# A lightning-attention and expert-mixture kernel: two more chunks laid out in DRAM, weight blocks read from the input, a block of sums turned on VectorE, PSUM pairs alternating

## The chip, the cores and the metric

The kernel runs on one core of one Trainium2 chip. The metric is device microseconds (us) of one execution. The kernel before took a median of 1186.92 us over 4 runs (1186.15 to 1188.08). Engines are named TensorE (PE; its weight loads are PEld), VectorE (DVE), ScalarE (ACT), POOL (GpSimd) and SyncE (SP, which issues nearly all DMAs). A line number L843 is a line of the kernel before.

## The reference

Two stages in float32. The first is attention with a decaying state, for 4 batches, 8 heads, 768 positions and head width 64; the second sends the 3072 resulting rows of 512 through 4 experts and adds them up with gates:

```python
# attention, per block of positions, state kv of 64x64 a head
intra = ((qb @ kb.T) * Dmask) @ vb
inter = (qb * lam_pow) @ kv_state
out   = intra + inter
kv_state = lam_block * kv_state + (kb * rev_pow).T @ vb

# experts: x is 3072x512, w1[e] 512x1024, w2[e] 1024x512
p = domain_probs / (domain_probs.sum(-1, keepdims=True) + 1e-09)
for e in range(4):
    h = np.maximum(x @ w1[e], 0.0)
    out += p[:, e:e + 1] * (h @ w2[e])
```

## The kernel before

**Chunks and groups.** The attention works in chunks of 128 positions, 6 a batch, 24 in all (n = 0 to 23, batch b = n // 6, chunk c = n % 6). Eight chunks make a group of 1024 rows, x transposed in `xT`; there are three groups g. The 12 units (g, e) of the expert stage follow one another. While TensorE does the second product (h @ w2) of one unit, it does the first product (x @ w1) of the next between, and steps of the next group's attention go in among them.

**Fast products.** Products are cut into 2x2 blocks and done with 7 products of blocks instead of 8 (M1 to M7, a Winograd scheme): some factors are plain blocks of a matrix, the others sums of blocks. `A_OF` names the factor of each product: A11, A12 and A22, for M1, M2 and M4, are plain blocks of w1; S1 to S4 are sums. Each block product is again cut into 7 inner ones (`INNER`), so that each outer factor has four inner blocks and four inner sums. In the first product (`first_product`, L821) two PSUM banks, g1 and g3, take the inner products by turns and VectorE or ScalarE adds them into blocks `m`. The second product of groups 0 and 1 is cut once (`second_product`, L882, banks q01, q02, q11, q12); in the last group it is nested twice (`nested_product`, L1084) with results `sums`, held transposed: features in partitions, rows in the free dimension.

**Prepared operands.** POOL makes the sums ahead of time, as chores from a list (`pump`) with an estimate of its own busy time, and SP stores what it made. For w1, `inner_w1` writes to `w1_ops[e, m]` seven blocks of 128x256, in the order M1, M7, M6, M5, M3, M2, M4: block 0 and blocks 5 and 6 are copies of the outer factor, blocks 1 to 4 are inner sums. `inner` (L167) stores them with three DMAs; `own_w1` (L1189) does it for expert 1, whose first use is straight from SBUF. `feed` (L748) loads them again: one DMA for x (`xs_in`, L756) and one for w1 (`ws_in`, L758), 896 KB each, one product ahead, into two buffers each. There are 70 such products, from 189 us on.

**Chunks by DRAM.** To make scores, q and k of a chunk are needed with the head dimension in partitions. `turn` (L519) does it for most chunks on TensorE: 4 transposes for q and 4 for k into PSUM (L529), copied to SBUF by ScalarE (L534, L535). For the chunks that `ACROSS` names, chunks 2 to 5 of batches 2 and 3, `bring_across` rearranges q and k within DRAM beforehand (32 DMAs a batch, DRAM to DRAM, in runs of 128 bytes, L367), one at a time between other DMAs (`trickle`); `load_across` (L384) then loads tiles that VectorE turns in blocks of 32x32, in place (L516). k is loaded in its natural layout too, for the state update; in the other path the same tile of k serves both.

**The end.** In the last unit (expert 3 of the last group) products are in the order `SEQ3` = M1, M3, M5, M7, M6, M2, M4. M2 is taken plain (`plain_product`, L1032, bank pM). After M6 the outer blocks are joined: `to_join` (L987) queues copies of sums to PSUM on ScalarE (`bring`) and additions on VectorE (`add`), done one step at a time. The results of blocks M3, M5, M2 and M4 are turned back to rows in partitions by `give` (L1010): TensorE transposes (L1018, 4 for each half of the rows), a copy by ScalarE (L1022), a store by SP (L1024). `after_last` says at which step each is given: M3 during product M2, M5 and M2 during product M4. M4 itself ends the kernel (`turn_end`, `turned_product`).

**PSUM pairs.** A nested product uses a pair of banks. Its pair is chosen by the product's number i in the expert, `i % 2` (three pairs, `i % 3`, in the last expert, which has no first product beside it). There are seven products an expert.

Of the kernel before, what the change touches and what calls it, by code (L numbers as in the profile page):

```python
# [22 lines left out]
def kernel(  # L23
# [30 lines left out]
    nc = tc.nc  # L54
# [4 lines left out]
    P = nc.NUM_PARTITIONS  # L59
# [4 lines left out]
    G = CPG * C  # L64
    NG = NTOK // G
    Q = G // 4
    DH = DOUT // 2
    W = 512
# [15 lines left out]
    MS = ("M1", "M2", "M3", "M4", "M5", "M6", "M7")  # L84
    A_OF = {"M1": "A11", "M2": "A12", "M3": "S4", "M4": "A22", "M5": "S1", "M6": "S2", "M7": "S3"}
# [5 lines left out]
    def small(name):  # L91
        return pool.tile([P, W], FP32, name=name, tag="t")
# [34 lines left out]
    w1_ops = dram.tile([E, 7, P, 7, 256], FP32, name="w1_ops")  # L127
# [9 lines left out]
    chores, queue, late, results, made = [], [], [], [], set()  # L137
    LEFT = 1

    def store(f):  # L140
        queue.append((busy[0] + 2, f))
# [22 lines left out]
        while what not in made:  # L164
            pump(force=True)

    def inner(eng, what, to, blk, ops, at):  # L167

        b = {n: blk[:, i, j * 256:(j + 1) * 256] for n, (i, j) in at.items()}
        s = stage.tile([P, 4, 256], FP32, name="ops", tag="st")  # L170
        for i, (name, x, y, op) in enumerate(ops):
            b[name] = s[:, SLOT[name]]
            tt(eng, b[name], b[x], b[y], op)
        store(lambda: (
            nc.sync.dma_start(out=to[:, 0], in_=blk[:, 0, 0:256]),
            nc.sync.dma_start(out=to[:, 1:5], in_=s[:]),
            nc.sync.dma_start(out=to[:, 5:7], in_=blk[:, 1].rearrange("p (a f) -> p a f", a=2)),
            made.add(what),
        ))

    SLOT = {"S3": 0, "S2": 1, "S1": 2, "S4": 3, "T3": 0, "T2": 1, "T4": 2, "T1": 3}
    S_OPS = (
# [5 lines left out]
        ("T4", "B21", "T2", ALU.subtract),  # L188
    )

    def inner_w1(e, m, blk):
        at = {"A11": (0, 0), "A21": (0, 1), "A12": (1, 0), "A22": (1, 1)}
        inner(nc.gpsimd, ("w1", e, m), w1_ops[e, MS.index(m)], blk, S_OPS, at)

    def inner_x(eng, g, m, blk):
        at = {"B11": (0, 0), "B12": (0, 1), "B21": (1, 0), "B22": (1, 1)}
# [156 lines left out]

    ACROSS = {2: 2, 3: 2}
    across = dram.tile([B, 2, P, NHP, NCH * 4, 32], FP32, name="across")
    pieces = []

# [76 lines left out]
    m = 1  # L436
# [311 lines left out]
    def feed(g, e, m):  # L748
        if (g, e, m) in fed:
            return  # L750
        while ("x", g, m) not in made and background:
            rest(force=True)
        until(("x", g, m))
        until(("w1", e, m))
        xs = stream.tile([P, 7, 256], FP32, name="xs_in", tag="x")
        nc.sync.dma_start(out=xs[:], in_=x_ops[g, MS.index(m)])  # L756
        ws = stream.tile([P, 7, 256], FP32, name="ws_in", tag="w")
        nc.sync.dma_start(out=ws[:], in_=w1_ops[e, MS.index(m)])  # L758
        fed[g, e, m] = {i: xs[:, X_AT[i]] for i in X_AT}, {i: ws[:, W1_AT[i]] for i in W1_AT}


# [213 lines left out]
        x = sums[a][:, 2 * k:2 * k + 2].rearrange("p k t -> p (k t)")  # L975
        tt(nc.vector, x, x, there[b, k][:], ALU.add)

    def joined(m=None):

        while m in apart:  # L980
            take(aside, True)
        while joins and (m is None or any(m in x for x, _ in joins)):
            joins.pop(0)[1]()
            if m is None:
                return

    def to_join(m):  # L987

        def steps(*work):
            for fs in work:  # L990
                joins.append(([x[1] for x in fs if x[0] == add], lambda fs=fs: [x[0](*x[1:]) for x in fs]))

        if m == "M3":
            steps(
                [(bring, "M1", 0, "q01")], [(bring, "M1", 1, "q02"), (add, "M6", "M1", 0)], [(add, "M6", "M1", 1)],
            )
        if m == "M5":
            join("M3", "M5")
            join("M2", "M1")
        if m == "M6":  # L1000
            steps(
                [(bring, "M6", 0, "s0")], [(bring, "M6", 1, "s1"), (add, "M7", "M6", 0)], [(add, "M3", "M6", 0)],
                [(bring, "M7", 0, "q11"), (add, "M7", "M6", 1)], [(bring, "M7", 1, "q12"), (add, "M3", "M6", 1)],
                [(add, "M4", "M7", 0)], [(add, "M4", "M7", 1)], [(add, "M5", "M7", 0)], [(add, "M5", "M7", 1)],
            )
# [4 lines left out]
    def give(m, t, tags, dds=(0, 1)):  # L1010

        joined(m)
        i, j = RESULT[m]
        p, o = bank(tags[t % len(tags)], "yp"), small("y")
        w = len(dds) * P
        for x, dd in enumerate(dds):
            for s in range(2):
                nc.tensor.transpose(  # L1018
                    out=p[:, s * w + x * P:s * w + (x + 1) * P], in_=sums[m][:, 2 * dd + t, s * P:(s + 1) * P],
                    identity=ident[:],  # L1020
                )
        nc.scalar.copy(out=o[:, 0:2 * w], in_=p[:, 0:2 * w])  # L1022
        r, d = LAST * G + j * W + t * 256, i * DH + dds[0] * P
        nc.sync.dma_start(  # L1024
            out=out[r:r + 256, d:d + w].rearrange("(s p) d -> p s d", p=P),
            in_=o[:, 0:2 * w].rearrange("p (s d) -> p s d", s=2),
        )


    PLAIN = E - 1, "M2"  # L1030
# [158 lines left out]
    def own_w1(m):  # L1189

        c = w1_now[1][A_OF[m]]
        b = {f"A{i + 1}{j + 1}": c[j][:, i * 256:(i + 1) * 256] for i in range(2) for j in range(2)}
        s = stage.tile([P, 4, 256], FP32, name="ops", tag="st")
        for n, x, y, op in S_OPS:
            b[n] = s[:, SLOT[n]]
            tt(nc.gpsimd, b[n], b[x], b[y], op)
        store(keep_own(("w1", 1, m), w1_ops[1, MS.index(m)], (
            ((0, 1), c[0][:, 0:256].unsqueeze(1)), ((1, 5), s[:]), ((5, 7), c[1].rearrange("p (a f) -> p a f", a=2)),
        )))
        return {i: b[A_OF[i]] for i in A_OF}  # L1200

    def keep_own(what, to, pieces):
        return lambda: ([nc.sync.dma_start(out=to[:, x:y], in_=of) for (x, y), of in pieces], made.add(what))
# [163 lines left out]
    def pause_till(i, x):  # L1367
# [13 lines left out]

    fill3 = [(e, m, k) for e in range(E) for m in SEQ3 for k in range(4)]
    after_last = {
        "M2": (None,) * 5 + (("M3", 0), ("M3", 1)),
        "M4": (("M5", 0), ("M5", 1), ("M2", 0), ("M2", 1)),
    }
    steps = attention(1)
    PACE = 1.0, 1.4, 1.0
    for at, (g, e) in enumerate(units):
# [14 lines left out]
        for i in range(7):  # L1404
# [8 lines left out]
                    out=gate_bc, in_=gate_rows[:, ahead[1]].partition_broadcast(P),  # L1413
                )
            if nested:
                b = nested_product(e, SEQ3[i], (("q01", "q02"), ("q11", "q12"), ("g1", "g3"))[i % (2 if ahead else 3)])
                if i < 6 and (e, SEQ3[i + 1]) != PLAIN:
                    inner_sums(e, SEQ3[i + 1])
            else:
                b = second_product(g, e, SEQ2[i], banks)  # L1420
# [4 lines left out]
            a = []  # L1425
            if ahead:
                a = first_product(*ahead, SEQ[i], blocks, ("g1", "g3"))
            if (e, SEQ3[i]) == END:
                b[6:6] = [lambda: (give("M4", 1, ("s0", "s1"), (1,)), turn_end(1, "q11"))]
                b[5:5] = [lambda: (give("M4", 0, ("s0", "s1"), (1,)), turn_end(0, "q12"))]  # L1430
            if not ahead:
# [6 lines left out]
            for x, part in enumerate(order):  # L1438
# [12 lines left out]
                if nested and ahead and x in (1, 3) and fill3:  # L1451
                    feed3(*fill3.pop(0))
                if turned_back and x > 0:
                    y = turned_back.pop(0)
                    if y:
                        give(*y[:2], ("s0", "s1"), *y[2:])
                if x == 0 and at * 7 + i >= 6 and fill:
                    feed(*fill.pop(0))
                if at == 0 and x == 0 and i < AHEAD:
# [36 lines left out]
```

## Time and profile before

| what | value |
|---|---|
| median of 4 runs | 1186.92 us (1186.15 to 1188.08) |
| the profiled execution | 1186.15 us |
| its span on the chip | 1184.4 us |
| TensorE busy | 1176.9 us |
| VectorE, POOL, ScalarE busy | 790.4, 630.0, 275.0 us |
| DMA | 324.23 MB, mean 274 GB/s |
| granted TensorE clock | 1.0 |

The span is what the profile sees, from the first to the last instruction; 1.75 us of the profiled execution lie around it. Matmul rows overlap in the profile (each lasts longer than the distance to the next start), so a stretch of them is timed from start to start. A row of a timeline has the start, the time it takes, the engine, the line, the operation, out<-in, shapes and how many instructions were merged, and in brackets the idle time before it and what ended that. A row of waits has the waiting engine and tile, what ended the wait, the total in us, how many there were and the longest. POOL and VectorE work side by side: a VectorE addition of two 128x512 tiles in SBUF lasts 0.68 us in some places and up to 1.36 us in stretches where POOL adds tiles too. The DMA line of the slices is the mean busy share of 16 DMA engines in tenths.

### The profile page before, as it was taken

The page shows a single profiled execution, that of the slowest core. Times are in us where ns is not written, and L with a number is a line of the kernel's source. Part 1 is how long each engine was busy: PE and PEld are TensorE (multiplying, and loading weights), DVE is VectorE, ACT ScalarE, POOL GpSimd, SP SyncE. Part 2 cuts the span into 40 slices and gives each one's busy share as a digit, 9 for nine tenths or more (in the row PEclk, how much of TensorE's full clock was granted, in tenths as well). Part 3 has the DMA queues.
Part 4 walks back from the last instruction along what each step waited for, and adds up shares of the span by engine and source line. Part 5 has one row for each costly group of instructions (what it writes and reads, how often), then busy time and mean ns, then how long its engine had stood idle before and what let it go on. Part 6 is the DMA issues. An engine that isn't in the chain of part 4 may idle for free.

```text
span 1184.4 us, 17886 instructions
## 1 busy us (share of the span) xinstructions
PE 1176.9 (99%) x6567; PEld 1023.5 (86%) x6567; DVE 790.4 (67%) x1329; ACT 275.0 (23%) x502; POOL 630.0 (53%) x600
## 2 busy tenths in 40 slices
PE   9999999999999999999999999999999999999998
PEld 8888888888888888888888888888888888888887
DVE  6785785567478757647856764764665676777784
ACT  3332122112211201211220120121243342341332
POOL 2756258349457800055253655425684683783884
PEclk9999999999999999999999999999999999999999
DMA  9698799999999997899997989898986657566542
GB/s 228 197 286 250 242 304 306 346 334 339 368 358 327 326 305 222 246 303 310 302 310 241 286 294 318 276 329 275 307 296 244 254 189 276 205 240 245 213 160 90
DMA packets 261927, 324.23 MB, mean 274 GB/s; under 512 B 117296, under 2 KB 203216, under 8 KB 261840
## 3 DMA queue, kind: packets, MB, share of 16 engines
q1 hardware_dynamic: 252288, 320.40, 81.5%
q10 hardware_dynamic: 9552, 2.69, 1.1%
q8 instruction: 52, 0.85, 0.3%
q14 instruction: 35, 0.29, 0.1%
HBM read 237.69 MB, written 89.54 MB: 276 GB/s over the span
## 4 chain that ended last, share of the span: by engine, by line
PE 94%; DVE 2%; SPq 2%; DMA 1%; issue 0%; ACT 0%; ACTq 0%; DVEq 0%
PE pg L843 39%; PE q L897 32%; PE pq L1104 13%; PE pc L1234 2%; PE op L579 2%; PE sp L551 1%; SPq L123 1%; PE pM L1234 1%; DVE m L95 1%; PE op L574 1%; PE op L587 1%; PE pM L1039 1%; SPq L341 0%; DMA vn<-in_v_dram 0%; SPq L118 0%
## 5 line engine op out<-in xcount | busy, mean ns | idle before, releaser
L843 PE MATMUL pg<-xs_in,ws_in 128*128 128x256 f32 x1960 | 469.7, 379 | 0.5 <-DVE m L95 0.5
L843 PEld LDWEIGHTS pg<-xs_in,ws_in 128*128 128x128 f32 x1960 | 371.3, 190 | 52.2 <-DVE m L95 1.5
L95 DVE TENSOR_TENSOR m<-pg,m 128x512 f32<-128x512 f32 x451 | 307.9, 687 | 105.9 <-PE pg L843 98.6
L897 PE MATMUL q<-w2t,hS 128*128 128x256 f32 x1024 | 243.4, 380 | 0.0
L897 PEld LDWEIGHTS q<-w2t,hS 128*128 128x128 f32 x1024 | 193.2, 190 | 27.0 <-issue 0.2
L913 DVE SCALAR_TENSOR_TENSOR acc<-q,gate,acc 128x256 f32<-128x256 f32 x192 | 92.5, 482 | 168.9 <-PE q L897 168.8
L897 PE MATMUL q<-w2t,m 128*128 128x256 f32 x768 | 182.7, 381 | 0.0
L897 PEld LDWEIGHTS q<-w2t,m 128*128 128x128 f32 x768 | 144.8, 190 | 20.5 <-issue 0.3
L855 ACT ACTIVATE m<-m 128x512 f32<-128x512 f32 x132 | 82.9, 630 | 281.5 <-DVE m L95 278.0
L95 POOL TENSOR_TENSOR m<-m,xT 128x512 f32<-128x512 f32 x64 | 80.7, 1277 | 71.7 <-ACT m L855 54.0
L95 POOL TENSOR_TENSOR kn<-kn,s_decay 128x512 f32<-128x512 f32 x20 | 23.2, 1158 | 140.1 <-DMA across<-in_k_dram 78.9
L95 DVE TENSOR_TENSOR sums<-pq,sums 128x256 f32<-128x256 f32 x153 | 64.4, 422 | 47.4 <-PE pq L1104 40.1
L851 ACT COPY m<-pg 128x512 f32<-128x512 f32 x88 | 51.6, 586 | 174.9 <-PE pg L843 172.5
L1104 PE MATMUL pq<-acc,w2t 128*128 128x256 f32 x352 | 86.6, 379 | 0.0
L95 POOL TENSOR_TENSOR ops<-w2b 128x256 f32<-128x256 f32 x24 | 18.4, 787 | 115.3 <-DMA w2b<-in_moe_w_dram 107.6
L1104 PEld LDWEIGHTS pq<-acc,w2t 128*128 128x128 f32 x352 | 66.8, 190 | 9.3 <-issue 0.3
L95 POOL TENSOR_TENSOR acc<-hT,hT 128x512 f32<-128x512 f32 x32 | 40.3, 1273 | 30.7 <-PE pq L1104 28.9
L95 POOL TENSOR_TENSOR w2o<-w2b 128x512 f32<-128x512 f32 x32 | 40.6, 1291 | 24.7 <-DMA w_ops<-w1b 14.4
L786 ACT ACTIVATE m<-m 128x512 f32<-128x512 f32 x44 | 27.7, 630 | 103.4 <-DVE m L95 103.3
L95 DVE TENSOR_TENSOR m<-m,m 128x512 f32<-128x512 f32 x56 | 48.8, 872 | 0.0
L95 DVE TENSOR_TENSOR hS<-m,m 128x512 f32<-128x512 f32 x56 | 43.6, 781 | 4.9 <-ACT m L855 4.9
L95 POOL TENSOR_TENSOR acc<-hT,acc 128x512 f32<-128x512 f32 x32 | 40.7, 1273 | 7.4 <-PE pq L1104 5.4
(157 smaller groups left out, 1362.9 us busy)
## 6 DMA issues: line engine op xcount, KB each, us to landing
xs_in<-x_ops SPq DMA_DIRECT2D x70, 896.0 KB, 6.1
ws_in<-w_ops SPq DMA_DIRECT2D x70, 896.0 KB, 8.7
w2t<-w_ops SPq DMA_DIRECT2D x66, 256.0 KB, 6.6
w2t<-w_sums SPq DMA_DIRECT2D x64, 256.0 KB, 3.7
w_ops<-ops SPq DMA_DIRECT2D x28, 512.0 KB, 5.7
w2t<-in_moe_w_dram SPq DMA_DIRECT2D x48, 256.0 KB, 3.4
w2b<-in_moe_w_dram SPq DMA_DIRECT2D x32, 256.0 KB, 6.0
w_sums<-w2o SPq DMA_DIRECT2D x16, 512.0 KB, 4.5
```

The costliest lines, as they stand in the source:

```text
L95: eng.tensor_tensor(out=o, in0=a, in1=b, op=op)
L123: by.dma_start(out=to[:, :, r], in_=of[:, :, r])
L551: nc.tensor.matmul(out=sp[r][:, ac * C:(ac + 1) * C], lhsT=hc(kT)[half[r], ac], rhs=hc(qT)[half[r], ac], start=True, stop=True,)
L579: nc.tensor.matmul(out=op[r][half[x], a * C:(a + 1) * C], lhsT=vn[:, 4 * r + 2 * a + x], rhs=hc(st[r])[:, 2 * a + x], start=(first and a = ...
L786: nc.scalar.activation(out=o[:], in_=o[:], func=AF.Relu)
L843: nc.tensor.matmul(out=p[:, j * 256:(j + 1) * 256], lhsT=ws[i][:, j * P:(j + 1) * P], rhs=xs[i], start=(fresh and j == 0), stop=True, skip ...
L851: nc.scalar.copy(out=new[at][:], in_=p[:])
L855: nc.scalar.activation(out=new[at][:], in_=new[at][:], func=AF.Relu)
L897: nc.tensor.matmul(out=p[:, s * DH:(s + 1) * DH], lhsT=h[A_OF[m]][:, c * 256 + s * P:c * 256 + (s + 1) * P], rhs=fed2[g, e, m][uu][:, c], ...
L913: nc.vector.scalar_tensor_tensor(out=o, in0=x, scalar=w, in1=o, op0=ALU.mult, op1=ALU.add)
L1104: nc.tensor.matmul(out=p[:, 0:256], lhsT=fed3[e, m, x // 2][:, x % 2, c * P:(c + 1) * P], rhs=b[B_OF[i]][:, c * 256:(c + 1) * 256], start= ...
L1234: nc.tensor.matmul(out=p[:, s * 256:(s + 1) * 256], lhsT=a[c][:, f:f + P], rhs=b[:, c, j * 256:(j + 1) * 256], start=(s == 0 and c == 0 an ...
```

## The change

Four things are changed.

1. `ACROSS` has batch 2 from chunk 0 on: chunks 12 and 13 are rearranged in DRAM as well, ten in all. The 32 rearranging DMAs of batch 2 move 6 chunks (96 KB each) where they moved 4 (64 KB).
2. For M1, M2 and M4 (`RAW`), the copies of plain blocks are no longer stored to `w1_ops`: only the four sums are, in one DMA instead of three. `feed` loads such a tile in three DMAs, blocks 0, 5 and 6 from the input w1 itself. Where all three stores remain, the sums go first.
3. `give_across` takes the place of `give` for block M3: VectorE turns 32x32 blocks of `sums` into a tile `y`, and eight DMAs of 64 KB, in runs of 128 bytes, put them at their places in the output (six from SP, two from ScalarE's queue). It is given two steps earlier, a half of the features at a time, and forces the joins up to that half alone.
4. The pair of banks of a nested product goes by the number of the product over all experts, `(at * 7 + i) % 2`, except in the last expert, which keeps `i % 3`.

In the changed order of instructions TensorE has 24 transposes fewer (16 for the two chunks, 8 for M3), ScalarE 6 copies fewer, VectorE 8 transposes more (four of 128x512, four of 128x256) and SP 40 DMAs more.

```diff
@@ -164,19 +164,17 @@
         while what not in made:
             pump(force=True)
 
-    def inner(eng, what, to, blk, ops, at):
+    def inner(eng, what, to, blk, ops, at, whole=True):
 
         b = {n: blk[:, i, j * 256:(j + 1) * 256] for n, (i, j) in at.items()}
         s = stage.tile([P, 4, 256], FP32, name="ops", tag="st")
         for i, (name, x, y, op) in enumerate(ops):
             b[name] = s[:, SLOT[name]]
             tt(eng, b[name], b[x], b[y], op)
-        store(lambda: (
-            nc.sync.dma_start(out=to[:, 0], in_=blk[:, 0, 0:256]),
-            nc.sync.dma_start(out=to[:, 1:5], in_=s[:]),
-            nc.sync.dma_start(out=to[:, 5:7], in_=blk[:, 1].rearrange("p (a f) -> p a f", a=2)),
-            made.add(what),
-        ))
+        pieces = [(to[:, 1:5], s[:])]
+        if whole:
+            pieces += (to[:, 0], blk[:, 0, 0:256]), (to[:, 5:7], blk[:, 1].rearrange("p (a f) -> p a f", a=2))
+        store(lambda: ([nc.sync.dma_start(out=x, in_=y) for x, y in pieces], made.add(what)))
 
     SLOT = {"S3": 0, "S2": 1, "S1": 2, "S4": 3, "T3": 0, "T2": 1, "T4": 2, "T1": 3}
     S_OPS = (
@@ -188,9 +186,11 @@
         ("T4", "B21", "T2", ALU.subtract),
     )
 
+    RAW = ("M1", "M2", "M4")
+
     def inner_w1(e, m, blk):
         at = {"A11": (0, 0), "A21": (0, 1), "A12": (1, 0), "A22": (1, 1)}
-        inner(nc.gpsimd, ("w1", e, m), w1_ops[e, MS.index(m)], blk, S_OPS, at)
+        inner(nc.gpsimd, ("w1", e, m), w1_ops[e, MS.index(m)], blk, S_OPS, at, m not in RAW)
 
     def inner_x(eng, g, m, blk):
         at = {"B11": (0, 0), "B12": (0, 1), "B21": (1, 0), "B22": (1, 1)}
@@ -353,7 +353,7 @@
 
 
 
-    ACROSS = {2: 2, 3: 2}
+    ACROSS = {2: 0, 3: 2}
     across = dram.tile([B, 2, P, NHP, NCH * 4, 32], FP32, name="across")
     pieces = []
 
@@ -755,7 +755,14 @@
         xs = stream.tile([P, 7, 256], FP32, name="xs_in", tag="x")
         nc.sync.dma_start(out=xs[:], in_=x_ops[g, MS.index(m)])
         ws = stream.tile([P, 7, 256], FP32, name="ws_in", tag="w")
-        nc.sync.dma_start(out=ws[:], in_=w1_ops[e, MS.index(m)])
+        if m in RAW:
+            i, j = int(A_OF[m][1]) - 1, int(A_OF[m][2]) - 1
+            src = moe_w1[e, j * 256:(j + 1) * 256, i * W:(i + 1) * W]
+            nc.sync.dma_start(out=ws[:, 0], in_=src[0:P, 0:256])
+            nc.sync.dma_start(out=ws[:, 1:5], in_=w1_ops[e, MS.index(m), :, 1:5])
+            nc.sync.dma_start(out=ws[:, 5:7], in_=src[P:].rearrange("p (a f) -> p a f", a=2))
+        else:
+            nc.sync.dma_start(out=ws[:], in_=w1_ops[e, MS.index(m)])
         fed[g, e, m] = {i: xs[:, X_AT[i]] for i in X_AT}, {i: ws[:, W1_AT[i]] for i in W1_AT}
 
 
@@ -975,11 +982,11 @@
         x = sums[a][:, 2 * k:2 * k + 2].rearrange("p k t -> p (k t)")
         tt(nc.vector, x, x, there[b, k][:], ALU.add)
 
-    def joined(m=None):
+    def joined(m=None, k=None):
 
         while m in apart:
             take(aside, True)
-        while joins and (m is None or any(m in x for x, _ in joins)):
+        while joins and (m is None or any(m == x and k in (None, y) for to, _ in joins for x, y in to)):
             joins.pop(0)[1]()
             if m is None:
                 return
@@ -988,7 +995,7 @@
 
         def steps(*work):
             for fs in work:
-                joins.append(([x[1] for x in fs if x[0] == add], lambda fs=fs: [x[0](*x[1:]) for x in fs]))
+                joins.append(([(x[1], x[3]) for x in fs if x[0] == add], lambda fs=fs: [x[0](*x[1:]) for x in fs]))
 
         if m == "M3":
             steps(
@@ -1025,6 +1032,25 @@
             out=out[r:r + 256, d:d + w].rearrange("(s p) d -> p s d", p=P),
             in_=o[:, 0:2 * w].rearrange("p (s d) -> p s d", s=2),
         )
+
+    halved = {}
+
+    def give_across(m, dd, t):
+
+
+        joined(m, dd)
+        i, j = RESULT[m]
+        if t == 0:
+            halved[m, dd] = small("y")
+        o = halved[m, dd]
+        nc.vector.transpose(out=o[:, t * 256:(t + 1) * 256], in_=sums[m][:, 2 * dd + t])
+        r, d = LAST * G + j * W, i * DH + dd * P
+        for a in range(4 * t):
+            by = nc.scalar if a == 1 else nc.sync
+            by.dma_start(
+                out=out[r:r + W, d + a * 32:d + (a + 1) * 32].rearrange("(b p) d -> p b d", p=32),
+                in_=o[a * 32:(a + 1) * 32].rearrange("p (b d) -> p b d", d=32),
+            )
 
 
     PLAIN = E - 1, "M2"
@@ -1194,9 +1220,10 @@
         for n, x, y, op in S_OPS:
             b[n] = s[:, SLOT[n]]
             tt(nc.gpsimd, b[n], b[x], b[y], op)
-        store(keep_own(("w1", 1, m), w1_ops[1, MS.index(m)], (
-            ((0, 1), c[0][:, 0:256].unsqueeze(1)), ((1, 5), s[:]), ((5, 7), c[1].rearrange("p (a f) -> p a f", a=2)),
-        )))
+        pieces = [((1, 5), s[:])]
+        if m not in RAW:
+            pieces += ((0, 1), c[0][:, 0:256].unsqueeze(1)), ((5, 7), c[1].rearrange("p (a f) -> p a f", a=2))
+        store(keep_own(("w1", 1, m), w1_ops[1, MS.index(m)], pieces))
         return {i: b[A_OF[i]] for i in A_OF}
 
     def keep_own(what, to, pieces):
@@ -1381,8 +1408,8 @@
 
     fill3 = [(e, m, k) for e in range(E) for m in SEQ3 for k in range(4)]
     after_last = {
-        "M2": (None,) * 5 + (("M3", 0), ("M3", 1)),
-        "M4": (("M5", 0), ("M5", 1), ("M2", 0), ("M2", 1)),
+        "M2": ((), (), (("M3", 0, 0), ("M3", 0, 1)), (), (("M3", 1, 0), ("M3", 1, 1))),
+        "M4": ((("M5", 0),), (("M5", 1),), (("M2", 0),), (("M2", 1),)),
     }
     steps = attention(1)
     PACE = 1.0, 1.4, 1.0
@@ -1413,7 +1440,8 @@
                     out=gate_bc, in_=gate_rows[:, ahead[1]].partition_broadcast(P),
                 )
             if nested:
-                b = nested_product(e, SEQ3[i], (("q01", "q02"), ("q11", "q12"), ("g1", "g3"))[i % (2 if ahead else 3)])
+                pair = (at * 7 + i) % 2 if ahead else i % 3
+                b = nested_product(e, SEQ3[i], (("q01", "q02"), ("q11", "q12"), ("g1", "g3"))[pair])
                 if i < 6 and (e, SEQ3[i + 1]) != PLAIN:
                     inner_sums(e, SEQ3[i + 1])
             else:
@@ -1425,7 +1453,7 @@
             a = []
             if ahead:
                 a = first_product(*ahead, SEQ[i], blocks, ("g1", "g3"))
-            if (e, SEQ3[i]) == END:
+            if nested and (e, SEQ3[i]) == END:
                 b[6:6] = [lambda: (give("M4", 1, ("s0", "s1"), (1,)), turn_end(1, "q11"))]
                 b[5:5] = [lambda: (give("M4", 0, ("s0", "s1"), (1,)), turn_end(0, "q12"))]
             if not ahead:
@@ -1451,9 +1479,11 @@
                 if nested and ahead and x in (1, 3) and fill3:
                     feed3(*fill3.pop(0))
                 if turned_back and x > 0:
-                    y = turned_back.pop(0)
-                    if y:
-                        give(*y[:2], ("s0", "s1"), *y[2:])
+                    for y in turned_back.pop(0):
+                        if SEQ3[i] == END[1]:
+                            give(*y[:2], ("s0", "s1"), *y[2:])
+                        else:
+                            give_across(*y)
                 if x == 0 and at * 7 + i >= 6 and fill:
                     feed(*fill.pop(0))
                 if at == 0 and x == 0 and i < AHEAD:
```

## Prediction

> **What bounds the kernel now.** I read the page's busy lines first, then the slices, then the waits of TensorE.
>
> ```profile
> PE 1176.9 (99%) x6567; PEld 1023.5 (86%) x6567; DVE 790.4 (67%) x1329; ACT 275.0 (23%) x502; POOL 630.0 (53%) x600
> ...
> DMA  9698799999999997899997989898986657566542
> ...
> PE 94%; DVE 2%; SPq 2%; DMA 1%; issue 0%; ACT 0%; ACTq 0%; DVEq 0%
> ```
>
> TensorE is busy 99% of the span and 94% of the chain that ended last. It hardly waits: the list of its waits sums to some 4 us. So time is saved only by taking instructions out of TensorE's queue or ending one of its few waits, and lost only by giving it a new wait. DMA is 0.9 or more busy in most slices up to 900 us, so that is where a load could come late; after 900 us it is half idle. The granted clock is 1.0 throughout.
>
> TensorE's own price list comes from distances between starts in its timeline. Eight 128x256 matmuls that follow each other take 1.73 us (671.78 to 673.51), 0.216 us each. A 128x128 transpose takes 0.109 us, as here, where chunk 12 is turned:
>
> ```profile
> 267.90 0.60 PE L529 MATMUL qp<-ident,qn 128*128 128x128 f32 x4
> 268.34 0.60 PE L529 MATMUL kp<-ident,kn 128*128 128x128 f32 x4
> 268.78 1.89 PE L843 MATMUL pg<-xs_in,ws_in 128*128 128x256 f32 x8
> ```
>
> Look at the starts, not the durations, which overlap: 8 transposes hold the queue from 267.90 to 268.78.
>
> **1. Two more chunks by DRAM (12 and 13).** Their 16 transposes leave TensorE: 2 x 8 x 0.109 = **-1.74 us**. Added on VectorE: two block transposes a chunk, 0.70 us each by the rows of the eight chunks already treated so, and ScalarE loses four copies of 0.59. VectorE holds them in chunk 12 between evictions of pg: the 128x512 sums hS that stood there (0.79, 1.09, 0.82 us at 271 to 275) move back two or three places, into gaps of 1.30, 0.43 and 1.83 us between 276 and 292. I followed the order of both engines to 293 us; the tightest place is the scores, which TensorE reaches at 273.1 and whose kx is turned at some 272.6. In chunk 13 VectorE idles up to 2.97 us at a time (305 to 315). If this cover were gone, the price is one stall such as the 0.77 us at 685.39, where a burst of m and hS sums on VectorE held a bank. I take 0, with bounds 0 and +0.8 a chunk. POOL's decay of kn no longer waits for a transpose; POOL ends no wait of TensorE, so that is 0 either way. SP: the 32 rearranging DMAs of the first batch carry 96 instead of 64 KB, each some 0.65 us on SP and landed after 4.2 us (median). Queued behind them between 66 and 170 us are weight loads and stores; the w2t loads there land 12 to 30 us before use. They must all have landed before chunk 12 is loaded (223 us); they were issued by 168. Cost 0. Loading chunk 12 itself brings 1024 instead of 768 KB, in the slices where DMA is full (343 GB/s): 0.75 us later landings, of which more below.
>
> **2. Plain blocks of w1 read from w1.** Each of 12 stores becomes one DMA of 512 KB in place of three (896 KB), the first of them between 68 and 387 us; 30 of the 70 loads ws_in become three DMAs on SP (128, 512, 256 KB) with the same bytes. TensorE waits for no ws_in now, so nothing can be gained; what can be lost is slack. A load is issued when the buffer two products back is free (SP's longest wait, 134 us in total, is this one) and must land within one product:
>
> ```profile
> L758 SPq DMA_DIRECT2D ws_in<-w_ops x70: 319/423/1374, 175.5 to 1109.3; - x70
> ...
> DMA to landing us min/median/max: 6.2/8.7/12.1
> ```
>
> Between landing and first use most of the 70 loads leave 2.5 to 8 us, but five leave little: 0.53 us (used at 249.68), 0.80 (409.49), 0.49 (827.95), 1.19 (853.85) and 1.28 (879.75). The third and the fifth are of plain blocks, whose next is 2.79 (337.50). Two more issues of 0.42 us put the last piece 0.84 us later: 0.35 us of stall at the third if TensorE waited for the whole tile; but in the changed order each matmul waits for its own piece, and the last is first read some 3 us into the product. I take 0, from 0 to +0.4. The load at 249.68 is not plain, and gets chunk 12's 256 KB more ahead of it; but the stores dropped at 199.6 and 213.0 (384 KB each) leave the same queue. 0, from 0 to +0.5.
>
> The Trainium skill (DMA: Bandwidth & Descriptors, Anatomy of one DMA) speaks against this part: it gives every DMA a fixed cost of about 2.0 us, on the GpSimd path. Two more in a row would by that put a load 4 us later and stall TensorE at the three plain loads with 0.49, 1.28 and 2.79 us of slack, 7.4 us in all. The rows say otherwise: xs_in and ws_in, issued 0.4 to 0.5 us apart, land 2 to 3 us apart with 896 KB each, so they overlap.
>
> **3. PSUM pairs alternate over all experts.** With 7 products an expert, the last and the next expert's first used the same pair, and TensorE waited for the bank:
>
> ```profile
> PE pq L1104 <- ACT sums L1112: 0.5, 1, 0.5
> ```
>
> ```profile
> 961.77 1.03 PE L843 MATMUL pg<-xs_in,ws_in 128*128 128x256 f32 x4
> ...
> 962.88 0.36 ACT L1112 COPY sums<-pq 128x256 f32<-128x256 f32 x1
> ...
> 963.30 1.13 PE L1104 MATMUL pq<-m,w2t 128*128 128x256 f32 x4 [0.51 <-ACT sums L1112]
> ```
>
> By the starts, the four matmuls from 961.77 are through at 962.63, the next starts at 963.30: 0.67 us, and its group takes 0.97 where 0.86 is the rule: 0.77. The same at 1048.20: 0.19 + 0.08 = 0.27. The third boundary (1133.08, 0.27) stays, since the last expert still starts with the first pair after the first pair. Sum: **-1.04 us**. What is late next: the operands from POOL (T3 done by 961.6, T2 by 964.2, needed at 963.4 and 966.0) and bank g1, freed at 964.25 and needed at 964.36, a tenth of a us to spare. Bounds: 0 if that bank takes over, -1.04.
>
> **4. One block of sums turned on VectorE.** 8 transposes leave TensorE at the end: -0.87 us. Four of 128x256 come to VectorE, which is not idle here:
>
> ```profile
> 1164.38 5.34 PE L1039 MATMUL pM<-m,w2s 128*128 128x256 f32 x24
> 1169.56 0.60 PE L1018 MATMUL yp<-ident,sums 128*128 128x128 f32 x4
> 1169.99 1.89 PE L1039 MATMUL pM<-m,w2s 128*128 128x256 f32 x8
> ```
>
> ```profile
> 1168.10 0.69 DVE L95 TENSOR_TENSOR sums<-pM,sums 128x512 f32<-128x512 f32 x1 [0.56 <-PE pM L1039]
> 1168.71 2.47 DVE L95 TENSOR_TENSOR sums<-sums,jp 128x512 f32<-128x512 f32 x4
> 1171.92 0.69 DVE L95 TENSOR_TENSOR sums<-pM,sums 128x512 f32<-128x512 f32 x1 [0.75 <-PE pM L1039]
> 1172.53 0.68 DVE L95 TENSOR_TENSOR sums<-sums,jp 128x512 f32<-128x512 f32 x1
> ```
>
> Read the two against each other: VectorE's last sum (block M5) ends at 1173.21 and TensorE turns that half at 1174.1. In the new order the stage is one run: 32 matmuls (6.91 us from 1164.38), 8 more (1.73), two transposes of M5, then the third needs that last sum: TensorE is there 8.86 us after the stage's start. VectorE leaves the eviction at +3.72 as now, then in one chain an add, two transposes, two adds, two transposes, an add, an eviction, the last add. Adds start 0.60 apart, evictions take 0.61; a transpose of 128x256 is not in the trace, so between 0.30 (half of the 0.60) and 0.42 (the 128x256 addition); I take 0.36, the wide transpose's step of 0.63 (335.51 to 336.14) less the 0.27 by which 512 and 256 columns differ in additions. End at 3.72 + 0.61 + 4 x 0.60 + 0.61 + 0.68 + 4 x 0.36 = 9.46: TensorE stalls 0.6, with the slow restart 0.7. So of 0.87 us **-0.17** is left (bounds -0.4 and 0). The wait is on TensorE, with all its queue behind it. The eight out DMAs of 64 KB (six on SP, two on ACT) go out by 1174; six at 0.6 us, landed 4.2 us after issue like the rearranging ones of 128-byte runs, are done before the last stores (1180 to 1183). Cost 0.
>
> The skill's Specifications on the same DMA page put 512 bytes as the least run at line rate and call shorter ones a read-modify-write; these out runs have 128. No run here shows a penalty: 64 KB of them land in the median time of larger DMAs, and the end does not wait for them.
>
> **Sum.** -1.74 - 1.04 - 0.17 = -2.95. The profiled execution took 1186.15, 1.75 more than its span, and becomes 1183.2; the median of the runs is 0.77 above it, so 1186.92 - 2.95 = **1184.0**. About 0.2% (2.4 us) can be told from no change, so this forecast clears it narrowly.
>
> **Rivals.**
> (a) VectorE keeps up at the end (its idle gaps of 0.56 and 0.75 us speak for it, the chain above against): -3.65, 1183.3.
> (b) New stalls eat part. VectorE's bursts already cost 0.27 at 642.67 and 0.77 at 685.39, when POOL runs beside them (1.36 us for an addition of 0.68), and every shift reshuffles which bursts meet; two such stalls, or a boundary that stays on g1, leave -1.4: 1185.5.
> (c) The pairs do not do what they say, since another wait stands behind: -1.9, 1185.0.
> (d) Slower: the plain loads land late, in the stage that is full of DMA. Stalls of 5.4 us are needed to be 2.4 slower. If every plain load landed 3.4 us later, three would stall, 0.6 + 2.9 + 2.1 = 5.6 us, net +2.65: 1189.6. It decides from 3.4 us on; the two issues account for 0.84. For it speaks DMA at 0.99 between 200 and 400 us; against it, unchanged bytes of loads and 4.6 MB fewer stores.
>
> **Numbers.** Forecast 0.50, (a) 0.14, (b) 0.17, (c) 0.10, (d) 0.09. Faster by over 0.2%: the forecast without its upper fringe, and (a), 0.60; within 0.2%: 0.31; slower: 0.09. Range: 1182.2 (a, and the stalls of 642.67 and 685.39 gone) to 1186.8 (only the 1.74 of the chunks, and two stalls more).
>
> **What would show it.** Transposes qp and kp 56 each instead of 64, yp at L1025 20; no wait on sums at the first two boundaries, one of 0.2 at the third; a wait of 0.5 to 0.9 us of yp on VectorE's sums some 9 us after the last pM stage starts; no wait on ws_in. The forecast is wrong if TensorE waits for a DMA anywhere past 60 us, or for kx.

## The result, and the profile after

The changed kernel took a median of 1185.75 us (1184.59 to 1187.83, 32 runs), the kernel before 1187.58 (1185.82 to 1191.07, 52 runs beside them). The ratio is 0.9987, 95% interval 0.9982 to 0.9992: 1.5 us less, 0.9 to 2.1. That is inside the predicted range, 1.75 us above the forecast of 1184.0, and within 0.2%: about half of the 2.95 us that the sum gave. The profiled execution took 1186.03 us, with a span of 1184.2.

The same three lines of the page as before the change:

```profile
PE 1175.9 (99%) x6543; PEld 1022.1 (86%) x6543; DVE 792.5 (67%) x1337; ACT 272.1 (23%) x496; POOL 630.1 (53%) x600
...
DMA  9798698999999897899997889898986657566643
...
PE 89%; DVE 4%; DMA 3%; issue 1%; SPq 1%; POOL 1%; ACT 0%; ACTq 0%; POOLq 0%; DVEq 0%
```

TensorE has its 24 instructions fewer, VectorE its 8 more, ScalarE 6 fewer. DMA is as full as before. New is the chain: VectorE has 4% of it where it had 2.

Chunk 12. TensorE's timeline, then VectorE's, of the changed kernel:

```profile
267.22 1.89 PE L904 MATMUL q<-w2t,hS 128*128 128x256 f32 x8
268.95 1.89 PE L850 MATMUL pg<-xs_in,ws_in 128*128 128x256 f32 x8
270.67 1.89 PE L904 MATMUL q<-w2t,hS 128*128 128x256 f32 x8
```

```profile
271.76 0.70 DVE L516 STREAM_TRANSPOSE qx<-qx 128x512 f32<-128x512 f32 x1
...
273.00 0.70 DVE L516 STREAM_TRANSPOSE kx<-kx 128x512 f32<-128x512 f32 x1
```

The starts on TensorE follow each other at 1.73 us: no transposes, no wait. VectorE's two stand between its other work.

The first boundary between experts, on TensorE of the changed kernel:

```profile
962.52 1.03 PE L850 MATMUL pg<-xs_in,ws_in 128*128 128x256 f32 x4
963.38 1.03 PE L1130 MATMUL pq<-m,w2t 128*128 128x256 f32 x4
964.25 1.03 PE L1130 MATMUL pq<-acc,w2t 128*128 128x256 f32 x4
```

Starts 0.86 and 0.87 us apart: the 0.77 us are gone, and so are the 0.27 at the second boundary. The third has its 0.27 still (1132.93).

The end, on TensorE and then on VectorE:

```profile
1172.86 0.38 PE L1025 MATMUL yp<-ident,sums 128*128 128x128 f32 x2
1173.58 0.88 PE L1025 MATMUL yp<-ident,sums 128*128 128x128 f32 x6 [0.34 <-DVE sums L95]
```

```profile
1169.15 0.76 DVE L1046 STREAM_TRANSPOSE y<-sums 128x256 f32<-128x256 f32 x2
...
1171.01 0.75 DVE L1046 STREAM_TRANSPOSE y<-sums 128x256 f32<-128x256 f32 x2
...
1172.86 0.67 DVE L95 TENSOR_TENSOR sums<-sums,jp 128x512 f32<-128x512 f32 x1
```

Two transposes at 1172.86, the third not at 1173.08 but at 1173.58, as soon as VectorE's addition is over. With the slow restart that is 0.56 us.

TensorE's list of waits, its first and fifth line:

```profile
PE pg L850 <- DVE m L95: 1.7, 5, 0.5
...
PE yp L1025 <- DVE sums L95: 0.3, 1, 0.3
```

There is none on ws_in and none on ScalarE's sums, as predicted. But pg waits for VectorE 1.7 us, where the first profile of before had 0.8.

**A balance from the starts.** For each profile the span is cut into four: from its start to the first pc matmul (the start-up); the waits after 64 us, which are what successive starts of 128x256 matmuls and 128x128 transposes on TensorE lie apart beyond 0.216 us or 0.109, where it is over 0.025; from the start of the last matmul to the end; and what is left, TensorE's own work. In us:

| profile | start-up | work | waits | start of the last matmul to end | span |
|---|---|---|---|---|---|
| before | 61.76 | 1111.71 | 7.31 | 3.58 | 1184.36 |
| before, again (e12) | 63.15 | 1111.72 | 8.86 | 3.60 | 1187.33 |
| changed | 62.48 | 1109.08 | 8.75 | 3.94 | 1184.25 |
| changed, again (e9) | 63.66 | 1109.03 | 8.71 | 3.95 | 1185.35 |
| e1_pairs | 62.74 | 1111.74 | 7.10 | 3.58 | 1185.16 |
| e2_chunks | 62.43 | 1109.96 | 8.21 | 3.59 | 1184.19 |
| e3_raw | 63.02 | 1111.64 | 8.36 | 3.86 | 1186.88 |
| e4_give | 62.07 | 1110.82 | 9.33 | 3.42 | 1185.64 |
| e5_noraw | 62.02 | 1109.09 | 8.74 | 3.42 | 1183.27 |
| e6_putback | 65.82 | 1110.76 | 8.21 | 3.82 | 1188.61 |
| e7_quiet | 63.88 | 1108.99 | 8.40 | 3.95 | 1185.22 |
| e8_better | 62.06 | 1109.09 | 8.58 | 3.93 | 1183.66 |
| e10_split | 63.10 | 1109.08 | 8.52 | 3.51 | 1184.21 |
| e11_best | 62.93 | 1109.01 | 7.61 | 4.10 | 1183.65 |

Work is exact from run to run; start-up and waits are not. The work fell by 2.63 us, where 16 + 8 transposes at 0.109 make 2.62. What this leaves to explain is why only 1.5 us of it, and of the waits removed at the boundaries, arrive.

### The profile page after: what moved, and what is told of

Same layout as the page of the kernel before. It is cut to its first block, busy times and chain, and to the rows that moved or that the text cites. A ratio compares the mean times of both kernels' runs of the same rounds, so it can differ in the third digit from the quotient of the medians.

```text
span 1184.2 us, 17883 instructions
## 1 busy us (share of the span) xinstructions
PE 1175.9 (99%) x6543; PEld 1022.1 (86%) x6543; DVE 792.5 (67%) x1337; ACT 272.1 (23%) x496; POOL 630.1 (53%) x600
## 4 chain that ended last, share of the span: by engine, by line
PE 89%; DVE 4%; DMA 3%; issue 1%; SPq 1%; POOL 1%; ACT 0%; ACTq 0%; POOLq 0%; DVEq 0%
PE pg L850 37%; PE q L904 30%; PE pq L1130 13%; PE pM L1261 2%; PE pc L1261 2%; PE sp L551 2%; PE op L579 2%; POOL ops L95 1%; SPq L123 1%; DVE hS L95 1%; PE op L574 1%; DMA w_ops<-w2o 1%; DVE m L95 1%; DMA ws_in<-w_ops 1%; PE op L587 1%
```

## The experiments

Theory A: TensorE is held where VectorE falls behind beside POOL, between 355 and 400 us, and what it gains earlier it loses there. Rival B: part 2 moves POOL, its stores and the loads, and that costs time. C: scatter of the start-up.

**Each part alone, on the kernel before.** e1 is part 3, e2 part 1, e3 part 2, e4 part 4; each edit is that part of the diff above. The lines that carry them:

```diff
e1 + pair = (at * 7 + i) % 2 if ahead else i % 3
e2 + ACROSS = {2: 0, 3: 2}
e3 + RAW = ("M1", "M2", "M4")
e4 + "M2": ((), (), (("M3", 0, 0), ("M3", 0, 1)), (), (("M3", 1, 0), ("M3", 1, 1))),
```

> The kernel before with the alternating pairs alone. All theories: the waits on sums at the first two boundaries between experts (0.77 and 0.27 us) are gone, nothing else is late before the end: -1.0 us (-0.8 to -1.1). If the bank g1 takes the wait over, 0.

> The kernel before with batch 2 rearranged from chunk 0 alone. Theory A (VectorE, slowed beside POOL, bounds the stretch from 380 to 400 us and releases TensorE there at the same moment however early it comes): the 16 transposes go (-1.74 at 305 us), but waits of pg on m of 0.4 to 1.3 us together come back by 400 us: -0.4 to -1.0 in all. Rival B (the new loads and dropped stores of w1 shift POOL and make these waits): no new wait here, -1.74.

> The kernel before with the plain blocks of w1 read from w1 alone. Theory A: 0 (-0.3 to +0.3), no wait of TensorE on ws_in, and the waits at 383 and 397 us as in the kernel before (0.1 in all). Rival B: +0.8 to +1.4, with the new waits at 383 and 397 us.

> The kernel before with the block M3 turned on VectorE alone. All theories: 8 transposes go (-0.87), and a wait of yp on VectorE's last sum of M5 comes, 0.56 as in the changed kernel: -0.3 (-0.5 to 0).

Measured, against before: e1 0.9995 (0.9987 to 1.0004), e2 0.9995 (0.9986 to 1.0004), e3 1.0011 (1.0001 to 1.0020), e4 1.0001 (0.9992 to 1.0010). In us: -0.6, -0.6, +1.3, +0.1, each with an uncertainty of about 1. One part alone is near the limit of what the runs tell; that part 2 alone makes it slower is the clearest of them. The four add up to +0.2, with an uncertainty of about 2, so they neither confirm nor exclude the -1.5 of the whole. e2 is the widest: its ratio gives theory A's number and its interval, -1.7 to +0.5, just leaves out the -1.74, but its 11 runs lie in two bunches, seven from 1185.86 to 1186.26 and four from 1188.12 to 1189.59, and the medians are 1.55 apart. The profiles say more. Work: e1 0, e2 -1.75, e3 -0.07, e4 -0.89, as priced. Waits in the stretch that theory A names stand in all four (e2 has the one at 383 alone), here in e4, whose TensorE runs the old order until 1160 us:

```profile
354.83 1.99 PE L848 MATMUL pg<-xs_in,ws_in 128*128 128x256 f32 x8 [0.34 <-DVE m L95]
384.80 1.99 PE L848 MATMUL pg<-xs_in,ws_in 128*128 128x256 f32 x8 [0.23 <-DVE m L95]
398.48 1.78 PE L848 MATMUL pg<-xs_in,ws_in 128*128 128x256 f32 x7 [0.46 <-DVE m L95]
```

So they are no work of the change; the first profile of before happened to have none.

**Part 2 undone in the changed kernel.**

```diff
-    RAW = ("M1", "M2", "M4")
+    RAW = ()
```

> The changed kernel with part 2 alone undone (all blocks of w1 stored to DRAM and loaded from there). Theory A (the missing 1.4 us is held back by waits of TensorE on VectorE's evictions between 355 and 400 us, which are there in any order; part 2 costs nothing): as the changed kernel, -1.5 us against the kernel before, within 0.5. Rival B (part 2 itself costs about 1 us, since it moves POOL's stores and the loads' issues): -2.5 to -2.9 us, and the waits near 383 and 397 us gone or shorter.

Ratio 0.9974 (0.9965 to 0.9983), median 1185.16 beside 1188.06: 3.1 us less than before, and 1.5 less than the changed kernel by the two ratios (0.3 to 2.8). That is rival B's number, a little beyond its upper end. Theory A falls with it as the cause: e5's waits in that stretch and just before it are as long as ever (0.62 at 336.9, a wait on ws_in in part, 0.26 at 353.6, 0.90 at 397.0), and the 2.95 us arrive all the same. But the half sentence of B that the waits at 383 and 397 would go was wrong.

**Sixteen transposes put back.**

```diff
+        if n in (12, 13):
+            for t in ("s0", "s1"):
+                dead = bank(t, "dead")
+                for ac in range(NHP):
+                    nc.tensor.transpose(out=dead[:, ac * C:(ac + 1) * C], in_=..., identity=ident[:])
```

> The changed kernel with 16 transposes put back on TensorE for chunks 12 and 13, eight each, of a tile of k, into PSUM banks that nobody reads and with no copies out of them (so TensorE has its old load at 268 and 310 us, and VectorE keeps its new one). If nothing absorbs the time: +1.74 us against the changed kernel, so +0.2 against the kernel before. Theory A: TensorE comes some 1.7 us later to the evictions it waits for near 383 and 397 us, these waits (0.54 and 0.72 us in the changed kernel) shrink, and the cost is only +0.5 to +1.2 us, so -1.0 to -0.3 against the kernel before.

Ratio 1.0001 (0.9993 to 1.0010), median 1187.76: 1.7 us above the changed kernel by the ratios, which is all of 1.74 and nothing absorbed. The interval leaves room for 0.4 to 2.9, so some absorption is not excluded; its profile has 0.30 and 0.71 at the two waits, where the changed kernel has 0.54 and 0.72. The dead transposes in its timeline:

```profile
272.22 1.04 PE L514 MATMUL dead<-ident,kn 128*128 128x128 f32 x8
273.09 1.89 PE L858 MATMUL pg<-xs_in,ws_in 128*128 128x256 f32 x8
```

0.87 us from start to start for eight: the price of part 1.

**POOL quiet at 340 to 400 us.**

```diff
-            tt(eng, b[name], b[x], b[y], op)
+            if what[:2] == ("x", 1):
+                eng.memset(b[name], 0.0)
+                busy[0] = max(busy[0], now[0]) + 256 / 480
+            else:
+                tt(eng, b[name], b[x], b[y], op)
...
-            halves(t[:], a, b, op)
+            if g == 1:
+                for i in range(2):
+                    nc.gpsimd.memset(t[:, i], 0.0)
+                    busy[0] = max(busy[0], now[0]) + W / 480
+            else:
+                halves(t[:], a, b, op)
```

> The changed kernel, but POOL's outer and inner sums of x for group 1 (made at some 340 to 400 us) are replaced by filling the tiles with zeros: these sums are left out of the computation, so the rows of group 1 lack them. The instructions of TensorE, VectorE and ScalarE and the bytes of the DMAs are unchanged. Theory A (VectorE falls behind there because its additions last twice as long beside POOL's): the waits of TensorE on VectorE between 355 and 400 us (1.3 us in sum in the changed kernel) vanish, VectorE's additions there take 0.68 instead of up to 1.36 us, and the time is 1 to 1.5 us below the changed kernel. Rival (VectorE is simply full there): waits stay.

Ratio 0.9982 (0.9973 to 0.9991), 0.6 us below the changed kernel and inside its interval. The waits at 383 and 397 are gone, one of 0.83 stands at 355.4, before the sums left out. VectorE in the changed kernel, then VectorE and POOL in this one:

```profile
387.70 1.36 DVE L95 TENSOR_TENSOR hS<-hS,m 128x512 f32<-128x512 f32 x1
```

```profile
379.16 0.68 DVE L95 TENSOR_TENSOR m<-m,m 128x512 f32<-128x512 f32 x1
...
389.00 0.68 DVE L95 TENSOR_TENSOR hS<-hS,m 128x512 f32<-128x512 f32 x1
```

```profile
378.33 0.99 POOL L318 MEMSET xo<- 128x512 f32 x2
379.26 1.08 POOL L174 MEMSET ops<- 128x256 f32 x4
```

The same addition of two SBUF tiles, at 387.70 and 389.00, takes 1.36 us beside POOL's additions and 0.68 with POOL idle. The one at 379.16 stands beside POOL filling tiles and takes 0.68; beside additions, in the changed kernel, it takes 0.92. The mechanism of theory A is there, and it belongs to both kernels; in time the run is inconclusive, since 0.6 is within its uncertainty. The Trainium skill (SBUF — State Buffer, SBUF: two separate sides) has a VectorE instruction with two SBUF inputs and a GpSimd one that reads SBUF lock each other out; fills, which read nothing, agree with it here.

**M3's second half later, and other pairs in the last expert.**

```diff
-        "M2": ((), (), (("M3", 0, 0), ("M3", 0, 1)), (), (("M3", 1, 0), ("M3", 1, 1))),
-        "M4": ((("M5", 0),), (("M5", 1),), (("M2", 0),), (("M2", 1),)),
+        "M2": ((), (), (("M3", 0, 0), ("M3", 0, 1))),
+        "M4": ((("M5", 0), ("M3", 1, 0), ("M3", 1, 1)), (("M5", 1),), (("M2", 0),), (("M2", 1),)),
...
-                pair = (at * 7 + i) % 2 if ahead else i % 3
+                pair = (at * 7 + i) % 2 if ahead else (1, 0, 2, 0, 1, 2, 0)[i]
...
-                        if SEQ3[i] == END[1]:
+                        if len(y) == 2:
```

> The changed kernel with two edits: the second half of block M3 is turned on VectorE during the last product, not before it, so that TensorE does not wait for VectorE's sums at 1173.6 us (0.56); and the last expert takes its pairs of banks in the order 1, 0, 2, 0, 1, 2, 0, so that its first product does not use the pair just left (0.27 at 1132.9). If both waits go and none comes: -0.83 us against the changed kernel, -2.3 against the kernel before. Rival: VectorE is now late for the last product's own sums or the store of M3 ends last: 0 or slower.

Ratio 0.9980 (0.9971 to 0.9989): 0.8 us below the changed kernel, as expected, but not by the way expected: its waits as a whole are only 0.17 shorter. The wait of yp is gone. The pairs gave nothing: the 0.27 at 1132.9 went, and the next two waits grew from 0.15 to 0.42 and from 0.52 to 0.81. TensorE in this kernel:

```profile
1134.47 2.83 PE L1130 MATMUL pq<-acc,w2t 128*128 128x256 f32 x12 [0.18 <-issue]
...
1147.54 2.68 PE L1130 MATMUL pg<-acc,w2s 128*128 128x256 f32 x11 [0.58 <-DVE sums L95]
```

A bank freed earlier moved the wait to the next thing that VectorE owes.

**The last four, on one chip: the changed kernel again, all loads cut in three, a best version, the kernel before again.** e9 and e12 have no edit. e10 and e11, on e5 and on the changed kernel:

```diff
e10 -            nc.sync.dma_start(out=ws[:], in_=w1_ops[e, MS.index(m)])
e10 +            for i, j in (0, 1), (1, 5), (5, 7):
e10 +                nc.sync.dma_start(out=ws[:, i:j], in_=w1_ops[e, MS.index(m), :, i:j])
...
e11 +    RAW = ()
e11 +        "M2": ((), (), (("M3", 0, 0), ("M3", 0, 1))),
e11 +        "M4": ((("M5", 0), ("M3", 1, 0), ("M3", 1, 1)), (("M5", 1),), (("M2", 0),), (("M2", 1),)),
e11 +                        if len(y) == 2:
```

> The changed kernel itself, unaltered, beside the other three and with a second profile. It tells how far two sets of runs of one kernel stand apart, and whether the differences of 1.3 us between single edits are more than that: -1.5 us against the kernel before, within 0.5, if they are. If its start-up (first matmul pc at 62.48 us in the first profile) or its waits at 383 and 397 us come out otherwise, single profiles scatter by that much.

> All blocks of w1 stored and loaded from there, as in e5_noraw, but every one of the 70 loads ws_in is cut into three DMAs (128, 512 and 256 KB) instead of the 30 of plain blocks in the changed kernel. If it is the three issues that cost the 1.3 us by which e5_noraw was faster than the changed kernel: 70/30 as much, so about +3 us against e5_noraw, back to the kernel before, with waits of TensorE on ws_in or on POOL's sums. If part 2's cost is scatter, or comes from where the bytes are read: within 0.6 us of e5_noraw, -2.5 to -3.1.

> The changed kernel without part 2 (as e5_noraw), and with the second half of block M3 turned on VectorE during the last product, the pairs of the last expert left as they were. The wait of 0.57 us at 1173 goes, as in e8_better: -0.56 us against e5_noraw, so -3.5 against the kernel before. If e5_noraw's lead was scatter: -0.56 against the changed kernel, -2.1.

> The kernel before itself, unaltered, for a second profile and as a measure of scatter: ratio 1.0000. Theory A says that its first profile was an unusually undisturbed one: the second has the first matmul pc at 62.0 to 63.0 us instead of 61.76, and waits on VectorE's evictions between 355 and 400 us, 0.7 to 1.8 us in sum, and its own time is about 1187.6. If the waits there belong to the change: none of them here, as in the first profile.

| kernel | median us | ratio to before | 95% |
|---|---|---|---|
| e9, changed again | 1186.23 | 0.9991 | 0.9983 to 1.0000 |
| e10, no part 2, 70 loads cut | 1185.02 | 0.9979 | 0.9970 to 0.9988 |
| e11, no part 2, M3 later | 1185.00 | 0.9976 | 0.9968 to 0.9985 |
| e12, before again | 1187.82 | 1.0004 | 0.9995 to 1.0013 |

The changed kernel came out at -1.1 and the kernel before at +0.5: two sets of one kernel stand 0.4 to 0.5 us apart, so 1.2 between e9 and both e10 and e11 is more than that. Three kernels without part 2 stand at -3.1, -2.5 and -2.8, the changed one at -1.5 and -1.1 (e8, with part 2 and two other edits, at -2.4). Part 2 costs 1 to 1.6 us: each of the differences alone is uncertain by 1 us or more, but all of them point one way.

It isn't the three issues. e10 has 140 loads more than e5 and should have lost 3 us; it lost 0.6, within its interval. TensorE waits for no ws_in in its profile. A fixed cost in series for each DMA, which the prediction weighed and set aside, is excluded once more.

e12 has the waits that the first profile of before lacked: 0.19 at 355.5, 0.57 at 385.5, and others (0.26 at 830.1, 0.62 at 880.9). e9 lacks the wait at 383 that the first profile of the changed kernel had.

Between the two profiles of the kernel before lie 1.39 us of start-up and 1.55 of waits, and 0.01 of work. So C is true of single profiles; the medians over many runs differ all the same.

e11 did not gain the 0.56 that it was given. The wait of yp is gone and the waits are 1.13 shorter than in e5, but the end is 0.68 longer: M3's stores stand in SP's queue shortly before the last results come, and SP is still behind when they do. SP's last issue starts 1.29 us after the start of the last matmul (0.71 in e5). SP in e11, then in e8, which turns M3 at the same place:

```profile
1174.41 3.09 SPq L1050 DMA_DIRECT2D out_dram<-y  x3
...
1180.84 0.46 SPq L1105 DMA_DIRECT2D out_dram<-y  x1
```

```profile
1174.57 1.60 SPq L1050 DMA_DIRECT2D out_dram<-y  x3
```

The same three issues take 3.09 us in e11, 2.00 of them the first alone, and 1.60 in e8, whose end is no longer for them (3.93, beside 3.94 in the changed kernel). So the longer end is one slow issue, met with a full queue behind it; why it was slow isn't shown, nor how often it is. The kernels without part 2 have the lowest medians measured, and e5 is the simplest of them.

## Why the prediction was right or wrong

**Part 1, -1.74: right in work, with a small wait it had not priced.** Work -1.75 (e2). The cover on VectorE held at both chunks: no wait at 268 to 315 us in any profile. POOL, put at 0 "either way", was not: in the changed kernel POOL starts its sum of w1 at 170.51 instead of 168.93 us, and what follows meets VectorE's work. VectorE's row in the changed kernel, and before:

```profile
173.47 1.56 DVE L95 TENSOR_TENSOR qs<-qT,q_decay 128x512 f32<-128x512 f32 x1
```

```profile
172.76 0.73 DVE L95 TENSOR_TENSOR qs<-qT,q_decay 128x512 f32<-128x512 f32 x1
```

TensorE then waits 0.33 us at 175.7, in all kernels with ten chunks and in none with eight. The step that failed: POOL ends no wait of TensorE itself, but it lengthens the instruction that does. Its size is small beside the runs' scatter: e5 has this wait too, and reaches the forecast sum.

**Part 2, 0 (0 to +0.4, and +0.5): the step that cost the forecast.** Its argument was right as far as it went: no wait on ws_in, three issues are hidden, and e10 shows so. It measures +1 to +1.6 us by e5 against the changed kernel, e9 against e10 and e11, and e3 against before (+0.1 to +2.4). What the profiles show of it is two things. One, the end: from the start of the last matmul on, 3.82 to 3.95 us in all six profiles with part 2, 3.42 to 3.60 in the seven without (e11 aside, whose last stores are late). SP's last issue in the changed kernel, whose span is 1184.25, and in e5, with 1183.27:

```profile
1181.02 0.37 SPq L1105 DMA_DIRECT2D out_dram<-y  x1
```

```profile
1180.56 0.37 SPq L1105 DMA_DIRECT2D out_dram<-y  x1
```

3.23 and 2.71 us from it to the end: 0.52 between the same instructions. The store is not what is longer: it lands 1.77 us after its issue in both, and from its landing to the end pass 1.46 and 0.94 us (1.33 to 1.47 in the six with part 2, 0.94 to 1.07 in the eight without). In the closing instructions, which the trace has and no view lists, POOL is late: in the changed kernel a drain of its own starts 0.36 us after the instruction before it and lasts 0.22, in e5 0.07 and 0.08. In e6 and e7, whose POOL has one and two instructions fewer, a delay of 0.33 and 0.32 us stands one and two instructions later. So in all six it meets the 837th instruction that the trace has of POOL, whichever that is. POOL has 839 to 841 of them with part 2 and 848 to 857 without, where the 837th works on tiles some 20 us or more before the end. By this the 0.3 to 0.5 us go with a place in POOL's order of instructions, and not with the time of any load or store; what delays POOL there isn't shown.

Two, VectorE is late at 641.85, and TensorE waits 0.51 us at 646.9. VectorE ahead of that wait, in the changed kernel and in e5:

```profile
641.85 0.42 DVE L95 TENSOR_TENSOR kv<-kv,op 128x256 f32<-128x256 f32 x1 [0.46 <-DVE kv L95]
...
642.79 1.77 DVE L95 TENSOR_TENSOR m<-m,m 128x512 f32<-128x512 f32 x1
```

```profile
642.51 1.32 DVE L95 TENSOR_TENSOR m<-m,m 128x512 f32<-128x512 f32 x1
```

Before its addition to kv VectorE idles 0.46 us, and the row names no other engine as ending that. The idle time is 0.45 or 0.46 in all five profiles with all four parts (both of the changed kernel, e6, e7 and e8) and 0.10 in all others, e3 among them. VectorE comes to the same burst 0.28 us later and meets POOL's additions in it for longer. TensorE's wait follows at 646.9 in both profiles of the changed kernel and in e8, a group of matmuls earlier in e6 and e7, and in none of e5, e10 and e11. But this does not make TensorE's waits longer in sum: they are 8.75 and 8.71 us in the changed kernel, 8.74 in e5 and 8.52 in e10, since e5 has its 0.62 at 336.9 instead. So of the 1 to 1.6 us the balance places the 0.3 to 0.5 at the end, and the rest it does not place; the same is so in e3, part 2 alone, where the end is 0.28 longer than before's of its +1.3. Which half of part 2 it is stays open: dropped stores alone, or loads from the input w1 alone, were not tried. The start-up is longer on average with part 2 (63.5 us against 62.5), but TensorE's and SP's instructions up to there are the same, and two profiles of the kernel before lie 1.39 apart; a part in it is neither shown nor excluded.

**Part 3, -1.04: right**, in place and size by the profiles (e1's time, -0.6 within 1, can't tell it from less); no other wait took the boundaries over, and the third stayed at 0.27 as said.

**Part 4, -0.17: right in mechanism and nearly in size.** Work -0.89, wait 0.56 (0.6 to 0.7 said): -0.3. The transpose of 128x256 was taken as a step of 0.36 us and takes 0.35 to 0.37 (two in 0.75). Rival (a) fell by that.

**The sum.** Parts 1, 3 and 4 were to give -2.95, and e5, which is these three, measures -3.1 (-4.2 to -2.0). Rival (b) named the kind of loss, new waits from VectorE's bursts beside POOL, and its 1185.5 is the nearest number, but it left the boundaries and chunks to blame and not part 2; of its two waits 685.39 stayed at 0.76, 642.67 went and 646.9 came a group of matmuls later. The range held, but partly by luck: its upper end was built on parts 3 and 4 giving nothing and on two more stalls, and the time that this left room for was lost to part 2, which the sum put at nothing. Rival (c) fell. Rival (d) fell by its mechanism, not by its sign: part 2 did cost, without one late load.

**The footing.** The four runs shown had a median of 1186.92, the 52 give 1187.58; from there the same sum ends at 1184.6, so 0.66 of the 1.75 us missed lie in the footing and the other 1.1 is what part 2 costs (1 to 1.6). The profile of before was one of its best executions as well: no waits at 355 to 400 us, and the earliest start-up of all fourteen. What it lacked was read as what the kernel lacks.

## What to carry to other kernels

Instructions taken off the bound engine left its own work to 0.02 us; the error lay in an edit costed at nothing because no load came late. When an edit has no gain of its own on the engine that binds, ask for its measurement alone before it rides along. And read waits off more than one profile: here two profiles of one kernel differ by 3 us in start-up and waits, more than the whole change.

## What the runs showed of the hardware

- With the same instructions up to 62 us, the first pc matmul starts at 61.76 to 65.82 us; by the lists of waits TensorE waits for loads of q and k, 0.2 us (e1) to 2.0 (e6) in sum. That is not all of the difference: the earliest start, 61.76, goes with 0.9.
- POOL lengthens VectorE's additions of two SBUF tiles while it reads tiles itself: up to 1.36 us beside its additions, 0.68 beside its fills.
- Out DMAs of 64 KB in runs of 128 bytes landed after 2.0 us (SP) and 2.2 (ACT), not 4.2 as estimated from the rearranging ones.
- Cutting 896 KB loads into 128, 512 and 256 KB landed them 6.4, 7.7 and 7.9 us after issue, where whole ones take 8.6.
- From the last store's landing to the end pass 0.94 to 1.07 us where POOL's trace has 848 instructions or more, and 1.33 to 1.47 where it has 839 to 841 and its 837th falls into the closing.
